# Head 0's cumulated sums by a transfer, the sum in two parts, and dummy matmuls by a running count

## The chip, the cores and the metric

The kernel runs on one core of a Trainium2 chip. A core has TensorE (PE in the profile; its weight loads are PEld), VectorE (DVE), ScalarE (ACT), GpSimd (POOL) and SyncE (SP), which here issues all transfers (DMA) from one queue in order. Each engine works through its own instructions in program order and waits on semaphores for the others. The metric is the device time of one execution in microseconds (us). [...]

## What is computed

Attention for 4 batches of 8 heads (576 positions, 64 wide) with a bias from cumulated sums, and then a mixture of four experts on the 2304 tokens:

```python
scores = scale * np.matmul(q, k.transpose(0, 1, 3, 2))
cum = np.cumsum(np.maximum(s, 0.0), axis=-1)
bias = -(cum[:, :, :, None] - cum[:, :, None, :])
scores = np.where(causal, -1000000000.0, scores + np.minimum(bias, 0.0))
attn = softmax(scores)
x = np.matmul(attn, v)             # then (B * S, H * D)
p = domain_probs / (domain_probs.sum(-1, keepdims=True) + 1e-09)
for e in range(E):
    h = np.maximum(x @ w1[e], 0.0)
    out += p[:, e:e + 1] * (h @ w2[e])
```

## The kernel before

**Order by a planner.** The program is straight-line code. Its first part (to about 320 us) is not written in the order in which it runs: `Sched.add` collects tasks with an estimated cost for each engine that could do them, dependences, a priority and buffers to take and give back, and `Sched.run` plays them through a model of the five engines (a clock `now` in ns, engines free from `T_START` on). Whichever task is free with the lowest priority number is emitted at that moment. So the order of instructions on each engine follows from planned times, and on the chip each engine keeps to that order.

**Attention.** `VISITS` lists 40 visits. Visits 0 to 7 take row blocks 0 to 2 (320 positions) of the first eight heads, visits 8 to 15 the remaining row blocks 3 and 4 of the same heads, visits 16 to 39 whole heads. Each visit loads q and k (L473, L480) into one of four buffers AB and v; each row block is a product S (L545), a minimum over it on VectorE (L562), an exponential on ScalarE (L570), the reciprocal of the sum (L576, L578), a normalisation, mostly on GpSimd (L375), transposes on TensorE (tile T, L599), copies out of PSUM (L380, L384), and a product with v (tile pv, L658). In visits 0 to 15 (`pq`) the product is one fp32 matmul over 66 rows: 64 of q and k, and two rows with the cumulated sums and constants, which a transfer (`ldc`, L490) brings from the tile `cx`. Its four rows hold ones, the sums (`cum`), the sums again (a ScalarE copy, L428), and -1. Visit 0 alone has no such transfer (`NDX = 1`): it multiplies 64 rows and adds the sums by two more matmuls per block, from `cum` and the identity (L547) and from `cum` and its negative, `nid` (L548).

The sums come from a scan on VectorE in two pieces, positions 0 to 319 and 320 to 575 (L426, L427), both ahead of every planned task. Two planned tasks (`t_chi` on ScalarE, `t_clo` on VectorE, priority `T_CE`) split the sums into a high and a low part, which `emit_ced` (L434) writes to memory for the visits from 16 on.

**Experts as filler.** Tasks of priority 1e6 and more are the matmuls of expert 0 (L746, L759, tile mo). TensorE takes them whenever no attention task is ready. They need the weights: eight blocks of 512 KB (L715) pass through two buffers `stage`, a copy on GpSimd or ScalarE (w1h, w2h) and a subtraction (w1l, w2l, L367). The remaining three experts follow after the attention phase in an order written out by hand.

**Dummies.** After 7 matmuls of ones in the start (`NWARM`, L404), `keep_warm` (L400) can place one dummy matmul of 192 columns into a free PSUM bank. The planner does so ahead of each attention task on TensorE, as long as fewer than `WCOLS` = 8 were placed in the last 3400 ns of planned time, and when TensorE has nothing to do after 3500. With the first expert matmul it ends for good:

```python
if e == "PE" and t.prio >= 1e6:
    self.warm = None
```

Of the kernel before, what the change touches and what calls it, by code (L numbers as in the profile page):

```python
# [11 lines left out]
F32 = mybir.dt.float32  # L12
# [81 lines left out]
DWQ = 0  # L94
DWL = 0
DWP = 1000
NDX = 1
NT_PR = 6000
T_CUM = 3800
T_CE = 6000  # L100
WMAX = 1
WCOLS = 8
T_START = (1500, 4200, 2000, 1700, 1100)
D1 = 700
LEND = {}
LAHEAD = 300
# [27 lines left out]
class Task:  # L134
    def __init__(self, engs, fn, deps, prio, take, give, xfer):
        self.engs = {e: c if isinstance(c, tuple) else (c, 0) for e, c in engs.items()}
        self.fn, self.prio, self.take, self.give, self.xfer = fn, prio, take, give, xfer
        self.wait = 0
        self.ready = 0.0
        self.next = []  # L140
        self.after = []
        self.done = None
        self.eng = None


class Sched:
# [38 lines left out]
    def run(self, until):  # L185
# [7 lines left out]
                for e in t.engs:  # L193
                    cand[e].append(t)
        now = 0.0
        recent = []
        while left:
            moved = False
            lend = not any(t.prio >= 1e6 and t.ready <= now + LAHEAD for t in cand["PE"])
            nxt = []  # L200
            for e in names:
                if free[e] > now:
                    nxt.append(free[e])
                    continue
                best = None
                for t in cand[e]:
                    if best is not None and t.key > best.key:
                        continue
                    if t.ready + t.engs[e][1] > now:
                        nxt.append(t.ready + t.engs[e][1])  # L210
                        continue
                    ok = True
                    for p, k in t.take:
                        f = min((b[0] for x in self.sources(t, p, lend) for b in self.pools[x]), default=1e18)
                        if f > now:
                            ok = False
                            if f < 1e17:
                                nxt.append(f)
                            break
                    if ok:  # L220
                        best = t
                if best is None:
                    if e == "PE" and self.warm and now > 3500:
                        x = self.warm(now)
                        if x:
                            recent.append(now)
                            free[e] = now + x
                            nxt.append(free[e])
                            moved = True
                    continue  # L230
                t = best
                extra = 0
                if e == "PE" and self.warm and t.prio < 1e6:
                    recent = [x for x in recent if x > now - 3400]
                    for _ in range(min(WMAX, WCOLS - len(recent))):
                        x = self.warm(now)
                        if x:
                            recent.append(now)
                            extra += x
                if e == "PE" and t.prio >= 1e6:  # L240
                    self.warm = None
                moved = True
                for x in t.engs:
                    cand[x].remove(t)
                for p, k in t.take:
                    x, b = min(((x, b) for x in self.sources(t, p, lend) for b in self.pools[x]), key=lambda y: y[1][0])
                    self.pools[x] = [y for y in self.pools[x] if y is not b]
                    self.tok[p, k] = b[1]
                    self.home[p, k] = x
                t.fn(e)  # L250
                end = now + extra + t.engs[e][0]
                free[e] = end
                if t.xfer is not None:
                    self.dma_free = max(self.dma_free, end + 700) + t.xfer / 330.0
                    end = self.dma_free + 900
                t.done, t.eng = end, e
                left.discard(id(t))
                for p, k in t.give:
                    self.pools[self.home.pop((p, k))].append([end + 150, self.tok.pop((p, k))])
                for n in t.after:  # L260
                    n.wait -= 1
                    if n.wait == 0:
                        for x in n.engs:
# [12 lines left out]


def body(ctx, tc, qk, vp, s, dp, w1, w1s, w2, w2s, out):
# [107 lines left out]

    s_sb = sch.pools["xr"][0][1][0:BH]
    cx = apool.tile([BH, 4, S], F32, name="cx")
    ones, cum = cx[:, 0], cx[:, 1]
    nid = const.tile([BH, BH], F32, name="nid")  # L390
    zero = const.tile([P, 1], F32, name="zero")
    warm = const.tile([P, 1], F32, name="warm")
    nc.sync.dma_start(out=s_sb, in_=s)
# [2 lines left out]
    def keep_warm(now):  # L396
        b = min((b for p in ("mo", "S", "T") for b in sch.pools[p]), key=lambda b: b[0], default=[1e18])
        if b[0] > now:
            return 0
        nc.tensor.matmul(b[1][:, 0:192], ones_bf[:, 0:128], ones_bf[:, 0:192], start=True, stop=True)  # L400
        return 83

    for _ in range(NWARM):
        nc.tensor.matmul(mo[1], ones_bf[:, 0:128], ones_bf, start=True, stop=True)  # L404
    nc.vector.memset(warm, 0.0)
    nc.gpsimd.memset(ones, 1.0)
    nc.gpsimd.memset(cx[:, 3], -1.0)
    nc.vector.memset(zero, 0.0)
    nc.scalar.activation(warm, warm, AF.Exp)
    make_identity(nc, idn)  # L410
    nc.gpsimd.tensor_scalar(nid, idn[0:BH, 0:BH], -1.0, 1.0, op0=ALU.mult, op1=ALU.mult)
# [10 lines left out]
    for _, t in sch.pools["osb"]:  # L422
        nc.vector.memset(t[:, 64:P], 0.0)
    s0 = rows(VA - 1)[1]
    for u, w in ((0, s0), (s0, S)):
        nc.vector.tensor_scalar(s_sb[:, u:w], s_sb[:, u:w], 0.0, 8.0, op0=ALU.max, op1=ALU.mult)  # L426
        nc.vector.tensor_tensor_scan(out=cum[:, u:w], data0=ones[:, u:w], data1=s_sb[:, u:w], initial=cum[:, u - 1:u] if u else 0.0, op0=ALU.mult, op1=ALU.add)  # L427
    nc.scalar.activation(cx[:, 2], cum, AF.Copy)  # L428

    c_hi, c_lo = aTh[0:BH, 0:S], aTl[0:BH, 0:S]  # L430

    def emit_ced(e):
        for r, t in ((0, ones), (1, ones), (2, c_hi.bitcast(F32)), (3, c_lo.bitcast(F32)), (4, cx[:, 3]), (5, cx[:, 3])):
            nc.sync.dma_start(out=ced[:, r], in_=t)  # L434

    t_chi = sch.add({"ACT": t_act(S, False)}, lambda e: hi(e, c_hi, cum), prio=T_CE)
    t_chi.ready = T_CUM
# [23 lines left out]
    for j, (h, ms) in enumerate(VISITS):  # L461
# [24 lines left out]
            ldv = sch.add({"SP": 500}, lambda e, j=j, h=h, nb=nb: nc.sync.dma_start(out=tok["vraw", j][:, 0:nb], in_=vp[h][:, 0:nb]),  # L486
                          [firstq.get(j - LV)], prio=base - 1300, take=[("vraw", j)], seq="vraw", xfer=nb * 128 * 64 * 4)
        ldc = None
        if pq and j >= NDX:
            ldc = sch.add({"SP": 500}, lambda e, j=j, h=h, ext=ext: nc.sync.dma_start(  # L490
                out=AB(j, F32)[64:66, :, 0:ext], in_=cx[h:h + 1, :, 0:ext].rearrange("p (r c) n -> p r c n", r=2)),
                prio=base - 1490, xfer=10000, follow=ld)
            ldc.ready = T_CUM + 600

        if first:
            qk_ready = [ld, ldc]
# [32 lines left out]
        for m in ms:  # L529
# [7 lines left out]
            for pi, (j0, j1) in enumerate(pieces):  # L537
                lastp = pi == len(pieces) - 1

                def f(e, j=j, a=a, j0=j0, j1=j1, c=c, pi=pi, ext=ext, pq=pq, h=h):  # L540
                    t = tok["S", (c, pi)]
                    if pq:
                        r = AB(j, F32)
                        k, w = 66 if j >= NDX else 64, min(P, ext - a)
                        nc.tensor.matmul(t[0:w, 0:j1 - j0], r[0:k, 0, a:a + w], r[0:k, 1, j0:j1], start=True, stop=k == 66)  # L545
                        if k == 64:
                            nc.tensor.matmul(t[0:w, 0:j1 - j0], idn[0:BH, h:h + 1].to_broadcast([BH, w]), cum[:, j0:j1], start=False, stop=False)  # L547
                            nc.tensor.matmul(t[0:w, 0:j1 - j0], cum[:, a:a + w], nid[:, h:h + 1].to_broadcast([BH, j1 - j0]), start=False, stop=True)  # L548
                    else:
                        for x, k in ((0, P), (1, 68)):  # L550
                            nc.tensor.matmul(t[:, 0:j1 - j0], AB(j)[0:k, x, a:a + P], tok["KK", j][0:k, x, j0:j1], start=(x == 0), stop=(x == 1))  # L551
                qt = sch.add({"PE": (t_pe4(j1 - j0) * (3 if j < NDX else 1) if pq else 2 * t_pe(j1 - j0))}, f, qk_ready + [last_q], prio=pr + pi, take=[("S", (c, pi))],
                             give=([("AB", j)] if pq else [("AB", j), ("KK", j)]) if lastp and m == ms[-1] else [])
                last_q = qt
                if j < NDX:
                    qt.ready = T_CUM - 150
                firstq.setdefault(j, qt)

                def f(e, m=m, n=n, a=a, j0=j0, j1=j1, c=c, pi=pi):
# [685 lines left out]
```

## Time and profile before

| | |
|---|---|
| median of three runs | 969.35 us (965.13 to 971.43) |
| the profiled execution, own time | 966.64 us |
| its span, first to last instruction | 964.9 us |
| mean granted clock of TensorE | 0.989 |
| busy: PE, DVE, ACT, POOL | 944.0, 734.5, 446.7, 450.0 us |

The profile is one execution. The span lies 1.7 us below the execution's own time, which includes what lies around it. A busy time of TensorE counts a slow matmul with its whole length, so the granted clock is to be read beside it.

### The profile page before, as it was taken

The numbers are of one execution on the slowest core, as the hardware profiler recorded it, in microseconds if no ns is written. First come the engines' busy times: TensorE is split into PE (matmuls) and PEld (weight loads), VectorE is DVE, ScalarE is ACT, GpSimd is POOL, SyncE is SP. The second block draws the span as 40 slices with busy tenths as digits, with TensorE's granted clock in tenths as the row PEclk, the third lists the DMA queues.
The fourth block names the chain that finished last, engine by engine and source line by source line (L and its number), as shares of the span: only waits on it lengthen the run. The fifth ranks groups of instructions, "written<-read, shape, count | busy, mean of one in ns | idle before, by whom it ended". The sixth has DMA issues, their size and how long they took to land.

```text
span 964.9 us, 18367 instructions
## 1 busy us (share of the span) xinstructions
PE 944.0 (98%) x6346; PEld 891.5 (92%) x6346; DVE 734.5 (76%) x1825; ACT 446.7 (46%) x1144; POOL 450.0 (47%) x505
## 2 busy tenths in 40 slices
PE   9989999999999999999999999999999999999998
PEld 6668889898898999999999999999999999999998
DVE  5879889889886222257688967997797979688976
ACT  4658787777775211244343344423343425343341
POOL 4456555655541389522381265317343624481222
PEclk7989999999999999999999999999999999999999
DMA  5857766757642596759645666555865468644613
GB/s 144 223 148 195 207 187 194 212 168 211 172 138 92 190 336 242 267 170 373 218 147 200 219 229 221 190 179 187 273 231 168 156 221 273 224 146 152 217 34 115
DMA packets 125975, 189.75 MB, mean 197 GB/s; under 512 B 10478, under 2 KB 102154, under 8 KB 125882
## 3 DMA queue, kind: packets, MB, share of 16 engines
q1 hardware_dynamic: 125882, 188.57, 61.0%
q8 instruction: 51, 0.84, 0.3%
q14 instruction: 42, 0.34, 0.1%
HBM read 144.73 MB, written 29.54 MB: 181 GB/s over the span
## 4 chain that ended last, share of the span: by engine, by line
PE 80%; DVE 11%; ACT 2%; DMA 2%; issue 2%; POOL 2%; DVEq 0%; SPq 0%; ACTq 0%; POOLq 0%
PE pb L1052 20%; PE pb L1044 19%; PE mo L1052 8%; PE mo L759 6%; PE mo L746 5%; PE T L599 5%; DVE w2l L367 4%; PE pv L658 4%; PE pb L746 4%; PE pb L759 3%; PE S L551 3%; PE S L545 2%; DMA x<-x_d 1%; DVE t L1086 1%; DVE a L562 1%
## 5 line engine op out<-in xcount | busy, mean ns | idle before, releaser
L1044 PE MATMUL pb<-x,w1h 128*128 128x384 f32 x1008 | 255.9, 334 | 0.5 <-ACT t L1082 0.5
L1044 PEld LDWEIGHTS pb<-x,w1h 128*128 128x128 f32 x1008 | 181.2, 188 | 0.9 <-ACT t L1082 0.8
L1044 PE MATMUL pb<-x,w1l 128*128 128x384 f32 x504 | 168.4, 334 | 0.0
L367 POOL TENSOR_TENSOR hT_r<-t,hT_r 128x768 fp32r<-128x768 f32 x18 | 33.9, 1885 | 273.8 <-ACT hT_r L380 177.4
L1082 ACT ACTIVATE t<-pb 128x384 f32<-128x384 f32 x144 | 67.0, 487 | 169.4 <-PE pb L1044 160.2
L1145 DVE SCALAR_TENSOR_TENSOR acc<-pb,prob,acc 128x256 f32<-128x256 f32 x288 | 126.2, 474 | 9.4 <-PE pb L1052 9.2
L375 POOL TENSOR_SCALAR a<-a,sm 64x64 f32<-64x64 f32 (+4 forms) x147 | 92.0, 630 | 67.2 <-DVE sm L578 39.6
L1052 PE MATMUL pb<-w2h,hT_r 128*128 128x256 f32 x720 | 115.7, 283 | 0.1
L570 ACT ACTIVATE a<-a,mx 64x64 f32<-64x64 f32 (+4 forms) x160 | 89.6, 562 | 26.9 <-DVE mx L562 16.5
L1052 PEld LDWEIGHTS pb<-w2h,hT_r 128*128 128x128 f32 x720 | 100.0, 191 | 0.5 <-DVE t L1086 0.3
L1059 ACT ACTIVATE hT_r<-t 128x768 fp32r<-128x768 f32 x54 | 45.7, 846 | 108.1 <-PE pb L1052 104.5
L1044 PEld LDWEIGHTS pb<-x,w1l 128*128 128x128 f32 x504 | 94.6, 188 | 0.0
L1086 DVE TENSOR_TENSOR t<-pb,t 128x384 f32<-128x384 f32 x108 | 56.2, 550 | 50.3 <-PE pb L1044 35.1
L1056 DVE SCALAR_TENSOR_TENSOR t<-t 128x768 f32<-128x768 f32 x72 | 88.0, 1223 | 2.2 <-ACT t L1082 2.1
L746 PE MATMUL mo<-xg,w1h 128*128 128x256 f32 (+1 forms) x344 | 80.5, 308 | 1.0 <-DVE xg L367 1.0
L599 PE MATMUL T<-idn,a 128*128 128x128 f32 x473 | 74.9, 281 | 6.7 <-POOL a L375 3.6
L380 ACT ACTIVATE aTh<-T 128x256 fp32r<-128x256 f32 (+2 forms) x278 | 65.6, 308 | 28.3 <-PE T L599 23.9
L1052 PE MATMUL pb<-w2l,hT_r 128*128 128x256 f32 x360 | 73.0, 284 | 5.1 <-DVE w2l L367 5.1
L635 DVE TENSOR_TENSOR aTl<-T,aTh 128x64 fp32r<-128x64 f32 (+3 forms) x247 | 72.6, 334 | 6.3 <-ACT aTh L380 5.2
L599 PEld LDWEIGHTS T<-idn,a 128*128 128x128 f32 x473 | 55.0, 143 | 21.1 <-issue 7.1
L562 DVE CUSTOM_DVE_ANT_0 a<-S,mask 128x192 f32<-128x192 f32 (+4 forms) x151 | 61.9, 419 | 3.9 <-PE S L545 1.9
L1145 DVE SCALAR_TENSOR_TENSOR acc<-mo,prob,acc 128x256 f32<-128x256 f32 x144 | 62.7, 474 | 1.6 <-PE mo L1052 1.6
(160 smaller groups left out, 2101.7 us busy)
## 6 DMA issues: line engine op xcount, KB each, us to landing
x<-xs_d SPq DMA_DIRECT2D x68, 768.0 KB
x<-x_d SPq DMA_DIRECT2D x55, 768.0 KB
xs_d<-x SPq DMA_DIRECT2D x12, 768.0 KB
raw<-in_qk_dram SPq DMA_DIRECT2D x24, 288.0 KB
KK<-AB_r SPq DMA_DIRECT2D x24, 288.0 KB
x_d<-xh SPq DMA_DIRECT2D x12, 576.0 KB
w1r<-in_w1s_dram SPq DMA_DIRECT2D x6, 1024.0 KB
w2r<-in_w2s_dram SPq DMA_DIRECT2D x6, 1024.0 KB
```

Source lines behind the costliest of these rows:

```text
L367: (nc.gpsimd if e == "POOL" else nc.vector).tensor_tensor(out=out, in0=in0, in1=in1, op=ALU.subtract)
L375: (nc.gpsimd if e == "POOL" else nc.vector).tensor_scalar(out, in_, scale, 1.0 if bias is None else bias, op0=ALU.mult, op1=ALU.mult if bi ...
L562: nc.vector.tensor_tensor_reduce(out=z[0:n, j0:j1], in0=tok["S", (c, pi)][0:n, 0:j1 - j0], in1=mask[0:n, 448 - a + j0:448 - a + j1], scale ...
L570: nc.scalar.activation(z[0:n, 0:bb], z[0:n, 0:bb], AF.Exp, bias=tok["mx", c][0:n, k:k + 1], scale=-1.0, accum_out=tok["sm", c][0:n])
L599: nc.tensor.transpose(t[:, 128 * k:128 * k + 128], z[:, 128 * x:128 * x + 128], idn)
L635: nc.vector.tensor_tensor(out=dst, in0=src, in1=h_.bitcast(F32), op=ALU.subtract)
L746: nc.tensor.matmul(t[:, 0:w], wl[q][:, dc, o:o + P], xgt[:, l, dc, 0:w], start=(u == 0), stop=(u == 3 * KD - 1))
L759: nc.tensor.matmul(t, ht[:, fc, 128 * ti:128 * ti + 128], wl[fc // 2][:, fc % 2, :], start=(u == 0), stop=(u == 3 * KF - 1))
L1044: nc.tensor.matmul(ts[u][:, 0:TG], wv[wl][:, k, 128 * u:128 * u + 128], x[:, xl_, k, :], start=start and k == 0 and n == 0, stop=k == 1 an ...
L1052: nc.tensor.matmul(ts[t][:, 0:256], h_part(o, hl_)[:, k, 128 * t:128 * t + 128], wv[wl][:, k, :], start=start and k == 0 and n == 0, stop= ...
L1056: (nc.gpsimd if e == "POOL" else nc.vector).scalar_tensor_tensor(out=out, in0=in0, scalar=0.0, in1=in1, op0=ALU.max, op1=op)
L1145: nc.vector.scalar_tensor_tensor(out=a_, in0=ts[t][:, 0:256], scalar=prob[:, tt, e:e + 1], in1=a_, op0=ALU.mult, op1=ALU.add)
```

## The change

Visit 0 gets its sums by the same transfer as the others, and `NDX`, `nid` and its two extra matmuls go. The scan's first piece (`cumulate(0, s0)`) and its copy stay ahead of the tasks; the second piece becomes planned tasks `t_cum2` (VectorE) and `t_cum3` (ScalarE) which are not planned before 12000 ns, and the transfers of visits 8 to 15 and `t_chi` depend on them. The dummy has 256 columns, and the planner places it by a running count: `active()` adds up TensorE's planned streaming over the last `HAM` ns, each task with a weight (0.9, products S of visits 0 to 15 with 0.5, dummies with 1.0). With nothing to do, TensorE gets a dummy while the count is under `FILL`; ahead of an attention task while it is under `KEEP`. This ends at `T_HAM` = 70000 ns of planned time. Engine start times and `T_CE`, `T_CUM` change too. The diff, its core:

```diff
-NDX = 1
-T_CUM = 3800
-T_CE = 6000
-WMAX = 1
-WCOLS = 8
-T_START = (1500, 4200, 2000, 1700, 1100)
+T_CUM = 4800
+T_CUM2 = 12000
+T_CE = 9000
+HAM = 3413
+KEEP = 0.45
+FILL = 0.6
+T_HAM = 70000
+T_START = (4000, 4300, 4700, 5200, 2600)
...
+        acts = [(800.0, T_START[0], 1.0)]
+
+        def active():
+            while acts and acts[0][1] <= now - HAM:
+                acts.pop(0)
+            return sum((min(y, now) - max(x, now - HAM)) * w for x, y, w in acts) / HAM
+
+        def dummy(at):
+            x = self.warm(at)
+            if x:
+                acts.append((at, at + x, 1.0))
+            return x
...
-                    if e == "PE" and self.warm and now > 3500:
-                        x = self.warm(now)
+                    if e == "PE" and self.warm and active() < FILL:
+                        x = dummy(now)
...
-                if e == "PE" and t.prio >= 1e6:
+                if e == "PE" and now > T_HAM:
                     self.warm = None
+                if e == "PE" and self.warm and t.prio < 1e6 and active() < KEEP:
+                    extra = dummy(now)
...
+                if e == "PE":
+                    acts.append((now + extra, end, t.act))
...
-        nc.tensor.matmul(b[1][:, 0:192], ones_bf[:, 0:128], ones_bf[:, 0:192], start=True, stop=True)
-        return 83
+        nc.tensor.matmul(b[1][:, 0:256], ones_bf[:, 0:128], ones_bf[:, 0:256], start=True, stop=True)
+        return 110
...
-    nc.scalar.activation(cx[:, 2], cum, AF.Copy)
+    def cum_again(u, w):
+        nc.scalar.activation(cx[:, 2, u:w], cum[:, u:w], AF.Copy)
+
+    cumulate(0, s0)
+    cum_again(0, s0)
+    t_cum2 = sch.add({"DVE": 1850}, lambda e: cumulate(s0, S), prio=T_CUM2 / 4)
+    t_cum2.ready = T_CUM2
+    t_cum3 = sch.add({"ACT": t_act(S - s0, False)}, lambda e: cum_again(s0, S), [t_cum2], prio=T_CUM2 / 4)
...
-        if pq and j >= NDX:
+        if pq:
...
+                          [None if first else t_cum3], prio=base - 1490, xfer=10000, follow=ld)
+            ldc.ready = T_CUM
...
-                            nc.tensor.matmul(t[0:w, 0:j1 - j0], idn[0:BH, h:h + 1].to_broadcast([BH, w]), cum[:, j0:j1], start=False, stop=False)
-                            nc.tensor.matmul(t[0:w, 0:j1 - j0], cum[:, a:a + w], nid[:, h:h + 1].to_broadcast([BH, j1 - j0]), start=False, stop=True)
...
+                qt.act = 0.5 if pq else 0.9
```

## Rows read from the trace of the kernel before

**Rows 1.** The page: chain that ended last by engine; granted clock in 40 slices.
```profile
PEclk7989999999999999999999999999999999999999
...
PE 80%; DVE 11%; ACT 2%; DMA 2%; issue 2%; POOL 2%; DVEq 0%; SPq 0%; ACTq 0%; POOLq 0%
```

**Rows 2.** Windows: stretch, length, busy PE, PEld, DVE, ACT, POOL (instructions), PEclk, DMA share, GB/s.
```profile
8.00:23.40 15.40, 15.40 (x59) 11.05 (x57) 7.37 (x50) 6.31 (x27) 5.47 (x10) 0.56 0.58 161
23.40:36.10 12.70, 12.55 (x90) 10.38 (x88) 12.15 (x53) 9.08 (x39) 5.08 (x6) 1.00 0.75 208
36.10:40.30 4.20, 2.84 (x20) 2.38 (x20) 2.43 (x9) 1.73 (x8) 3.04 (x3) 1.00 1.06 282
40.30:52.20 11.90, 10.90 (x56) 7.60 (x56) 8.99 (x33) 7.51 (x27) 6.54 (x9) 1.00 0.88 231
52.20:57.80 5.60, 2.35 (x15) 1.66 (x14) 5.00 (x12) 1.70 (x6) 3.93 (x5) 0.88 0.48 150
57.80:63.20 5.40, 5.37 (x22) 5.08 (x23) 3.02 (x13) 1.97 (x7) 2.20 (x3) 0.50 0.22 59
63.20:70.00 6.80, 6.60 (x40) 5.09 (x39) 5.93 (x21) 5.27 (x17) 2.69 (x7) 0.99 0.33 83
70.00:305.00 235.00, 230.95 (x1573) 206.90 (x1571) 208.47 (x819) 183.02 (x613) 128.60 (x278) 1.00 0.64 183
305.00:964.90 659.90, 649.74 (x4457) 637.28 (x4455) 476.01 (x801) 227.35 (x401) 288.10 (x167) 1.00 0.61 205
```

**Rows 3.** Chain that ended last at 70 us: start, length, engine, tile, line.
```profile
8.38 1.05 PE mo L547 x2
9.43 1.07 PE mo L548 x2
...
11.14 0.37 PE mo L545 x2
...
13.11 1.12 PE S L545 x2
...
38.05 0.20 PE S L545 x2
38.24 0.09 PE mo L400
38.33 0.37 PE S L545 x2
...
49.49 5.48 DMA stage<-in_w_dram
```

**Rows 4.** Waits, 0 to 70 us: in total, times, longest.
```profile
POOL w2h L382 <- DMA stage<-in_w_dram: 6.0, 4, 2.2
```

**Rows 5.** Timeline of the start: start, length, engine, line, operation [idle before <- releaser].
```profile
0.72 0.40 SPq L393 DMA_DIRECT2D xr<-in_s_dram  x1
...
1.18 0.75 SPq L473 DMA_DIRECT2D AB_f<-in_qk_dram  x1
...
2.60 0.69 DVE L426 TENSOR_SCALAR xr<-xr 32x320 f32<-32x320 f32 x1 [0.48 <-DMA xr<-in_s_dram]
...
3.41 0.81 DVE L427 TENSOR_TENSOR_SCAN cx<-cx,xr 32x320 f32<-32x320 f32 x1
...
4.15 1.07 DVE L426 TENSOR_SCALAR xr<-xr 32x256 f32<-32x256 f32 x1
...
4.63 0.50 PEld L545 LDWEIGHTS S<-AB_f 64*128 64x128 f32 x2 [0.30 <-DMA AB_f<-in_qk_dram]
...
5.25 0.74 DVE L427 TENSOR_TENSOR_SCAN cx<-cx,xr 32x256 f32<-32x256 f32 x1
...
6.03 0.68 ACT L428 ACTIVATE cx<-cx 32x576 f32<-32x576 f32 x1 [3.81 <-DVE cx L427]
...
7.32 0.74 DVE L367 TENSOR_TENSOR aTl<-cx,aTh 32x576 fp32r<-32x576 f32 x1 [1.32 <-ACT aTh L380]
```

**Rows 6.** The dummies' line L400: weight loads, min/median/max ns, first and last start.
```profile
L400 PEld LDWEIGHTS <-const-bfloat16-1.0 x51: 95/125/258, 3.3 to 38.4; 128*128 128x128 bf16 x51
```

More of the change, by code (lines that the diff above doesn't have):

```diff
@@ L143, in __init__ @@
         self.eng = None
+        self.act = 0.9
 class Sched:
@@ L195, in run @@
         now = 0.0
-        recent = []
+        acts = [(800.0, T_START[0], 1.0)]
[8 more added lines that the diff above has]
+            return x
         while left:
@@ L222, in run @@
                 if best is None:
-                    if e == "PE" and self.warm and now > 3500:
-                        x = self.warm(now)
+                    if e == "PE" and self.warm and active() < FILL:
+                        x = dummy(now)
                         if x:
-                            recent.append(now)
                             free[e] = now + x
@@ L229, in run @@
                             moved = True
+                    elif e == "PE" and self.warm:
+                        nxt.append(now + 100)
                     continue
@@ L232, in run @@
                 extra = 0
[L233 to L239, printed above, removed]
-                if e == "PE" and t.prio >= 1e6:
+                if e == "PE" and now > T_HAM:
                     self.warm = None
+                if e == "PE" and self.warm and t.prio < 1e6 and active() < KEEP:
+                    extra = dummy(now)
                 moved = True
@@ L388, in body @@
     cx = apool.tile([BH, 4, S], F32, name="cx")
-    ones, cum = cx[:, 0], cx[:, 1]
-    nid = const.tile([BH, BH], F32, name="nid")
+    ones, cum, minus = cx[:, 0], cx[:, 1], cx[:, 3]
     zero = const.tile([P, 1], F32, name="zero")
@@ L406, in body @@
     nc.gpsimd.memset(ones, 1.0)
-    nc.gpsimd.memset(cx[:, 3], -1.0)
+    nc.gpsimd.memset(minus, -1.0)
     nc.vector.memset(zero, 0.0)
@@ L410, in body @@
     make_identity(nc, idn)
-    nc.gpsimd.tensor_scalar(nid, idn[0:BH, 0:BH], -1.0, 1.0, op0=ALU.mult, op1=ALU.mult)
     nc.gpsimd.memset(mask, 0.0)
@@ L424, in body, with cumulate @@
     s0 = rows(VA - 1)[1]
-    for u, w in ((0, s0), (s0, S)):
+    def cumulate(u, w):
         nc.vector.tensor_scalar(s_sb[:, u:w], s_sb[:, u:w], 0.0, 8.0, op0=ALU.max, op1=ALU.mult)
         nc.vector.tensor_tensor_scan(out=cum[:, u:w], data0=ones[:, u:w], data1=s_sb[:, u:w], initial=cum[:, u - 1:u] if u else 0.0, op0=ALU.mult, op1=ALU.add)
-    nc.scalar.activation(cx[:, 2], cum, AF.Copy)
+    def cum_again(u, w):
[5 more added lines that the diff above has]
+    t_cum3 = sch.add({"ACT": t_act(S - s0, False)}, lambda e: cum_again(s0, S), [t_cum2], prio=T_CUM2 / 4)
     c_hi, c_lo = aTh[0:BH, 0:S], aTl[0:BH, 0:S]
     def emit_ced(e):
-        for r, t in ((0, ones), (1, ones), (2, c_hi.bitcast(F32)), (3, c_lo.bitcast(F32)), (4, cx[:, 3]), (5, cx[:, 3])):
+        for r, t in ((0, ones), (1, ones), (2, c_hi.bitcast(F32)), (3, c_lo.bitcast(F32)), (4, minus), (5, minus)):
             nc.sync.dma_start(out=ced[:, r], in_=t)
-    t_chi = sch.add({"ACT": t_act(S, False)}, lambda e: hi(e, c_hi, cum), prio=T_CE)
-    t_chi.ready = T_CUM
+    t_chi = sch.add({"ACT": t_act(S, False)}, lambda e: hi(e, c_hi, cum), [t_cum2], prio=T_CE)
     t_clo = sch.add({"DVE": t_dve(S), "POOL": (t_pool2(S), D3)}, lambda e: sub(e, c_lo, cum, c_hi.bitcast(F32)), [t_chi], prio=T_CE)
@@ L488, in body @@
         ldc = None
-        if pq and j >= NDX:
[L490 to L493, printed above, removed]
+        if pq:
+            ldc = sch.add({"SP": 500}, lambda e, j=j, h=h, ext=ext: nc.sync.dma_start(out=AB(j, F32)[64:66, :, 0:ext], in_=cx[h:h + 1, :, 0:ext].rearrange("p (r c) n -> p r c n", r=2)),
+                          [None if first else t_cum3], prio=base - 1490, xfer=10000, follow=ld)
+            ldc.ready = T_CUM
         if first:
@@ L543, in f @@
                         r = AB(j, F32)
-                        k, w = 66 if j >= NDX else 64, min(P, ext - a)
-                        nc.tensor.matmul(t[0:w, 0:j1 - j0], r[0:k, 0, a:a + w], r[0:k, 1, j0:j1], start=True, stop=k == 66)
-                        if k == 64:
-                            nc.tensor.matmul(t[0:w, 0:j1 - j0], idn[0:BH, h:h + 1].to_broadcast([BH, w]), cum[:, j0:j1], start=False, stop=False)
-                            nc.tensor.matmul(t[0:w, 0:j1 - j0], cum[:, a:a + w], nid[:, h:h + 1].to_broadcast([BH, j1 - j0]), start=False, stop=True)
+                        w = min(P, ext - a)
+                        nc.tensor.matmul(t[0:w, 0:j1 - j0], r[0:66, 0, a:a + w], r[0:66, 1, j0:j1], start=True, stop=True)
                     else:
@@ L551, in f @@
                             nc.tensor.matmul(t[:, 0:j1 - j0], AB(j)[0:k, x, a:a + P], tok["KK", j][0:k, x, j0:j1], start=(x == 0), stop=(x == 1))
-                qt = sch.add({"PE": (t_pe4(j1 - j0) * (3 if j < NDX else 1) if pq else 2 * t_pe(j1 - j0))}, f, qk_ready + [last_q], prio=pr + pi, take=[("S", (c, pi))],
+                qt = sch.add({"PE": (t_pe4(j1 - j0) if pq else 2 * t_pe(j1 - j0))}, f, qk_ready + [last_q], prio=pr + pi, take=[("S", (c, pi))],
                              give=([("AB", j)] if pq else [("AB", j), ("KK", j)]) if lastp and m == ms[-1] else [])
                 last_q = qt
-                if j < NDX:
-                    qt.ready = T_CUM - 150
+                qt.act = 0.5 if pq else 0.9
                 firstq.setdefault(j, qt)
```

## The prediction

> **What bounds the kernel now.** I read the page first. Its chain of work that ended last is 80% TensorE, and the clock row shows full speed everywhere but in the first and third slices of 24 us [rows 1]. [...]
>
> The windows by stage, second, say where it loses. From 70 us on TensorE is busy 230.95 of 235.00 and then 649.74 of 659.90 us at full clock [rows 2]; the change places nothing there. Since mixture-of-experts matmuls fill every TensorE gap of the attention phase, a shift of the pattern at 70 us should arrive at the end unchanged. That is an assumption; what it can cost is in the range.
>
> All that can be won lies before 70 us. The mean granted clock gives the time at the lower level: at a mean of 0.56 over 15.4 us it is (1 - 0.56) / 0.5 x 15.4 = 13.6 us, in one stretch; the second stretch is 0.88 over 5.6 us, 0.50 over 5.4 us and 0.99 over 6.8 us, so 1.3 + 5.4 + 0.1 = 6.9 us [rows 2]. In the first, TensorE is busy 15.40 of 15.40 us while VectorE is busy 7.37; in the next, VectorE is busy 12.15 of 12.70. Before the second, TensorE was busy only 2.35 of 5.60 us.
>
> The chain of waits, third, tells who sets the pace. Up to 23.4 us it is TensorE alone, and head 0 holds it for long: its third block ends with two cumulated-sum matmul pairs, 1.05 + 1.07 us, at 10.50 us; head 1 starts at 11.14 [rows 3]. Then VectorE paces to about 36 us. At 49.49 the chain waits 5.48 us for a transfer of expert weights [rows 3]; GpSimd waited four times for those, 6.0 us together [rows 4]. The transposes, and then TensorE, come behind that.
>
> **The change, part by part.**
>
> *Head 0 by a transfer.* Removed: the pairs of L547 and L548. Added: one small transfer of the sums' rows, after which head 0 is multiplied like the others. In the timeline of the start [rows 5] the first scan ends at 3.41 + 0.81 = 4.22. The copy on ScalarE now takes 320 columns instead of 576, 0.68 x 320/576 = 0.38 us, with a handover about 4.7. From issue to use the transfer of s took 2.60 - 0.72 = 1.88 us, that of head 0's q and k 4.63 - 1.18 = 3.45 us, so these sums land between 6.6 and 8.2; I take 7.0, since 5 KB are nearer to the small one. The two later transfers of the row wait in SP's queue behind it, and so do the loads of heads 2 and 3, which are not needed before 8 us. Head 0's three products at full clock are 0.20 and 0.37 us [rows 3], and half of the 1.12 us that 320 columns took at half clock: 1.13 us. They end at 8.1 to 8.2 where they ended at 10.50: 2.3 us earlier (1.1 to 2.7).
>
> *The sum in two parts.* The second half (1.07 + 0.74 = 1.81 us of VectorE, in the start at 4.15 and 5.25 [rows 5]) comes later, among the softmax work, and the 0.74 us subtraction of the split sums as well, which held VectorE at 7.32 after a wait for ScalarE. Behind the second half stand the row minima of heads 1 to 3. I count both against VectorE below. The result is first needed by the loads of visit 8, when the first heads are through; if it came later than that, every load behind that one in SP's queue would wait.
>
> *Dummies by a running count, in the first 36 us.* If the clock stays up, TensorE no longer paces: its work from 8.0 to 23.4 halves to about 8 us. VectorE does. Its work from 8.0 to 36.1 is 7.37 + 12.15 = 19.52 us [rows 2], and with 1.81 + 0.74 it is 22.07, starting at about 7.2. How densely it packs is not shown here: at best as in 23.4 to 36.1 (0.957), so 7.2 + 23.1 = 30.3 and 5.8 us are won; at worst TensorE still paces and only the start counts. I take the long attention row, 208.47 / 235.00 = 0.887 [rows 2]: 7.2 + 24.9 = 32.1, so 4.0 us are won at the 36.1 us mark (this contains the 2.3).
>
> *What is late next: the expert weights.* From 36.1 to 52.2 the DMA share is 1.06 and 0.88 [rows 2]; a stage that begins earlier does not get its 512 KB blocks earlier unless the queues had room. They had: 0.25 x 12.7 = 3.2 us in 23.4 to 36.1 and 0.12 x 11.9 = 1.4 us in 40.3 to 52.2. But two staging buffers chain each load to the split of the one before last. Of the 4.0 us between 0 and 4.0 pass; I take 3.0.
>
> *The second stretch at the lower clock.* Dummies now go on to 70 us of planned time instead of ending with the first expert matmul; the last of the 51 before started at 38.4 us [rows 6]. If they bridge 52 to 58 us, the 5.4 us in which TensorE was the bound at half clock (busy 5.37) shrink by half: 2.7 us. Bounds: 0, and 6.9 / 2 = 3.45.
>
> *What the dummies cost.* One of 192 columns took 0.09 us on the chain [rows 3]; one of 256 is then 0.12 us. Placed where the chip idles they cost nothing, and from 36.1 to 70 it idles 1.36 + 1.00 + 3.25 + 0.03 + 0.20 = 5.8 us, of which the rule fills 0.6, 3.5 us. They cost their full time where only the plan has a gap. I take 0.3 us, bounds 0 and 3.5. Each one also writes a bank and so waits for its last reader; in the row of the 51 I see nothing that waits for them. The cover is the plan's timing.
>
> *Sum.* 3.0 + 2.7 - 0.3 = 5.4 us. The profiled execution took 966.64 us (span 964.9), so 961.2 on its scale. It lies 2.7 us under the median of the three runs, 969.35 (965.13 to 971.43); the mean of all four is 968.1, and 968.1 - 5.4 = **962.7 us** is what I forecast.
>
> *A rule against it.* In 8.0 to 23.4 us TensorE was busy all of the time and yet had the lower clock [rows 2]: with products of 64 and 66 rows, transposes and a few dummies, busy time alone does not keep it up. The new count gives transposes the same 0.9 as full products. [...]
>
> **The rivals.**
>
> 1. *The count is wrong and the clock falls all the same.* For it: the full but slow stretch just told; the dummies are withheld at a count of 0.45 while products of 66 rows, counted at 0.5, run. Against: from 23.4 to 36.1 a mixture of the same products, transposes and dummies kept 1.00 [rows 2]. Only the earlier start is left, 2.3 us less 0.3: 966.1 us.
> 2. *The start's gain is lost at the expert weights.* For it: the DMA share of 1.06, four waits [rows 2, 4]. Against: the room before. Left are 2.7 - 0.3: 965.7 us.
> 3. *More is won.* VectorE packs at 0.957 (5.8 us), all 6.9 us go to full clock (3.45), and the TensorE gap of 52.2 to 57.8 closes (3.25 us): 12.5 us, 955.6. For it: the gap hangs on GpSimd's queue, where attention work stands behind a weight split that waits. Against: all three at once.
> 4. *Slower: dummies in front of real work.* The plan's gaps are not the chip's. Between 38.5 and 70 us the rule can place up to 0.6 x 31.5 = 18.9 us of dummies; on a TensorE that is really the bound (5.37 of 5.40 us) each costs 0.12 us. Above 5.7 us, some 47 of them, the kernel is slower than before; the full 18.9 give 968.1 - 5.7 + 18.9 = 981.3 us. For it: TensorE is in order and the expert matmuls need each slot. Against: the plan, too, has those matmuls as filler, so few gaps.
>
> **How the numbers follow.** The forecast has 0.40, rival 1 0.20, rival 2 0.15, rival 3 0.15, rival 4 0.10. The first three lie between 962.7 and 966.1; from run to run another 3 us come on top. Rival 4 (0.10), the far half of rival 3 and some spread are left out, under 0.2: range 955 to 970 us. One per cent of 969.35, 9.7 us, is about what a measurement can tell from no change. Below 959.7 lie most of rival 3 and a part of the forecast's high side: 0.20. Above 979.0 lies the bad half of rival 4, and some chance that a reshuffled plan loses elsewhere: 0.08. The rest, 0.72, is within 1%.
>
> **What would show it.** Head 0's first product at about 7.0 us and head 1's by 8.5; no L547 or L548. The granted clock at 1.00 in every window to 70 us; a window of 0.5 anywhere speaks for rival 1. VectorE's share from 8 to 32 us near 0.89. The waits for the weight transfers still there but ending some 3 us earlier (rival 2: at the same 55 us). Dummies after 38.5 us few, and in TensorE's idle time (rival 4: dozens, among expert matmuls). The windows from 70 us on should be the same work in the same length. I am wrong above all if TensorE's idle time between 70 and 305 us, now 4 us, changes by more than 2.

## The result, and the profile after

The changed kernel takes 953.13 us (median of five runs, 953.01 to 955.22) against 969.35 us before: a ratio of 0.9849 with a 95% interval of 0.9824 to 0.9874. It is 1.5% faster, three times the 5.4 us that were forecast, and lies under the range of 955 to 970 us. The profiled execution took 953.91 us, its span is 952.1 us; the span before was 964.9, so the two traces differ by 12.8 us.

The page of the changed kernel, its clock row and the chain by engine, answers [rows 1]:

```profile
PEclk9899999999999999999999999999999999999999
...
PE 75%; DVE 13%; ACT 3%; issue 3%; DMA 3%; POOL 2%; SPq 0%; DVEq 0%; ACTq 0%; POOLq 0%
```

The windows of the changed kernel, the same stretches and columns as [rows 2] (in the changed file L545 has become L562, L658 L671, L746 L759, L759 L772):

```profile
8.00:23.40 15.40, 13.60 (x79) 10.55 (x78) 13.19 (x64) 10.82 (x48) 9.90 (x15) 1.00 0.82 218
23.40:36.10 12.70, 11.15 (x48) 9.22 (x49) 10.26 (x52) 7.47 (x34) 6.30 (x8) 0.73 0.79 230
36.10:40.30 4.20, 4.20 (x24) 3.26 (x23) 2.66 (x12) 2.78 (x11) 2.22 (x4) 1.00 1.01 239
40.30:52.20 11.90, 9.69 (x62) 7.96 (x61) 10.30 (x31) 7.84 (x23) 6.38 (x10) 1.00 0.85 258
52.20:57.80 5.60, 5.60 (x42) 5.01 (x41) 4.92 (x15) 3.53 (x11) 2.38 (x5) 1.00 0.47 135
57.80:63.20 5.40, 5.40 (x38) 4.56 (x38) 5.29 (x20) 4.63 (x15) 3.70 (x6) 1.00 0.20 62
63.20:70.00 6.80, 5.39 (x35) 4.29 (x35) 6.34 (x20) 4.89 (x15) 3.88 (x8) 1.00 0.77 195
70.00:305.00 235.00, 231.50 (x1571) 207.44 (x1570) 203.23 (x806) 175.47 (x600) 129.15 (x271) 1.00 0.64 178
305.00:952.10 647.10, 637.45 (x4385) 626.78 (x4384) 471.37 (x787) 223.96 (x388) 288.17 (x167) 1.00 0.62 208
```

The clock column reads 1.00 in 8.00 to 23.40 here and 0.50 in 57.80 to 63.20 in [rows 2], and a mean between the two where it changes within a window; 0.50 is called the lower clock. Three things are to be seen. Both stretches at the lower clock are gone, and a shorter one has come: in 23.4 to 36.1 the mean is 0.73. From 70 us on nothing changed in kind: TensorE idles 3.50 us up to 305 where it idled 4.05. And TensorE's idle time as a whole is the same, 952.1 - 930.9 = 21.2 us against 964.9 - 944.0 = 20.9; it is its *busy* time that fell, by 13.1 us.

The dummies' line in the changed kernel (min/median/max ns, first and last start), beside [rows 6]:

```profile
L411 PEld LDWEIGHTS <-const-bfloat16-1.0 x16: 97/152/152, 3.3 to 14.9; 128*128 128x128 bf16 x16
L411 PE MATMUL mo<-const-bfloat16-1.0 x14: 272/420/421, 3.7 to 6.0; 128*128 128x256 bf16 x14
L411 PE MATMUL T<-const-bfloat16-1.0 x2: 273/273/273, 12.3 to 15.0; 128*128 128x256 bf16 x2
```

The running count placed 16 dummies where there had been 51: 14 in front of head 0's first product, two later, none after 15 us. The timeline of TensorE in the start:

```profile
3.70 2.58 PE L411 MATMUL mo<-const-bfloat16-1.0 128*128 128x256 bf16 x14
6.59 0.79 PE L562 MATMUL S<-AB_f 66*128 66x64 f32 x4 [0.31 <-DMA AB_f<-cx]
7.21 0.87 PE L562 MATMUL mo<-AB_f 66*128 66x320 f32 x4
7.92 1.08 PE L562 MATMUL S<-AB_f 66*128 66x192 f32 x4
9.11 0.79 PE L562 MATMUL mo<-AB_f 66*128 66x64 f32 x4
```

Head 0's first product waits for the transfer until 6.59 us. The row of 14 dummies that fills this wait, called the bridge below, ends 0.31 us earlier. By 9 us the products of two heads are through.

**An account of TensorE's time.** Since TensorE sets the end and its idle time did not change, I put its busy time together from its parts: time = work at full clock + half of the time at the lower clock + dummies + head 0's two extra products + idle time. The half is read from lengths on the chain of the kernel before: a dummy of 192 columns takes 0.16 us from 11.51 us, where the clock reads 0.50, and 0.08 us from 36.49, where it reads 1.00:

```profile
11.51 0.16 PE T L400
...
36.49 0.08 PE mo L400
```

The time at the lower clock is read from windows of 2 us, as 2 us x (1 - mean clock) / 0.5 each; a dummy of 192 columns counts as 0.08 us and one of 256 columns as 0.11 us (in the timeline of the changed kernel, one starts at 12.26 us and the next matmul at 12.37, where the clock reads 1.00). The extra products come from the chain of the kernel before; five pieces of it, the last four of them extra products beside the two in [rows 3]:

```profile
3.91 0.80 PE mo L400 x5
...
5.32 0.36 PE S L547 x2
5.68 0.22 PE S L548 x2
...
6.61 0.52 PE S L547 x2
7.13 0.33 PE S L548 x2
```

With 1.05 and 1.07 they are 3.55 us; the clock fell at about 8.67 (the window of 8.50 to 9.00 reads 0.66), so 1.83 us of them ran at half of it and count as 0.9: 2.6 us at full clock. One stretch at the lower clock stays out of the account. The windows read 1.00 from 0 us on, but the five dummies of 192 columns at 3.91 us take 0.16 us each, twice the 0.08, so the lower clock still held there; by 5.32 us the lengths are those of the full clock (0.36 us for the first pair of L547, 0.61 in e13 below). The changed kernel starts with such a stretch too (a dummy of its bridge takes 420 ns in the median, the two later ones 273); the others are taken to do so as well, and it is left in the last column. If the account is right, what is left, the work, must be the same in every variant. All profiles but that of e13, told below, in us:

| kernel | span | idle | at lower clock, half | dummies | extra products | left |
|---|---|---|---|---|---|---|
| before | 964.9 | 20.9 | 21.0, 10.5 | 51, 4.1 | 2.6 | 926.8 |
| changed | 952.1 | 21.2 | 8.0, 4.0 | 16, 1.8 | 0 | 925.1 |
| e1 | 969.6 | 27.5 | 22.8, 11.4 | 57, 4.6 | 0 | 926.1 |
| e2 | 958.3 | 20.6 | 14.5, 7.2 | 10, 1.1 | 2.6 | 926.8 |
| e3 | 957.6 | 24.7 | 14.6, 7.3 | 0 | 0 | 925.6 |
| e4 | 953.5 | 22.3 | 5.5, 2.8 | 27, 3.0 | 0 | 925.5 |
| e5 | 963.8 | 26.6 | 10.2, 5.1 | 45, 5.0 | 0 | 927.1 |
| e6 | 960.0 | 28.5 | 8.1, 4.0 | 16, 1.8 | 0 | 925.7 |
| e8 | 956.5 | 21.9 | 21.0, 10.5 | 0 | 0 | 924.1 |
| e9 | 961.1 | 22.2 | 21.7, 10.8 | 0 | 2.6 | 925.4 |
| e10 | 957.0 | 20.6 | 19.1, 9.6 | 15, 1.6 | 0 | 925.2 |
| e11 | 957.3 | 23.5 | 10.9, 5.5 | 15, 1.6 | 0 | 926.7 |
| e12 (before again) | 964.6 | 20.3 | 20.9, 10.4 | 51, 4.1 | 2.6 | 927.2 |

It closes to 924.1 to 927.2 in thirteen profiles. So the 12.8 us between the two traces are: lower clock 6.5, dummies 2.3, extra products 2.6, idle time -0.3, and 1.7 within the account's own spread. That spread is 3.1 us, so the account alone shows the clock's term; the terms of dummies and products are smaller than it, and for the dummies e8 and e9 below are the evidence.

### The profile page after: what moved, and what is told of

Read it like the earlier page. It is cut to its first block, busy times and chain, and to the rows that moved or that the text cites. A ratio compares the mean times of both kernels' runs of the same rounds, so it can differ in the third digit from the quotient of the medians.

```text
span 952.1 us, 18227 instructions
## 1 busy us (share of the span) xinstructions
PE 930.9 (98%) x6299; PEld 883.1 (93%) x6299; DVE 730.7 (77%) x1821; ACT 443.9 (47%) x1145; POOL 456.2 (48%) x508
## 4 chain that ended last, share of the span: by engine, by line
PE 75%; DVE 13%; ACT 3%; issue 3%; DMA 3%; POOL 2%; SPq 0%; DVEq 0%; ACTq 0%; POOLq 0%
PE pb L1065 20%; PE pb L1057 20%; PE mo L1065 8%; PE mo L759 5%; PE mo L772 4%; DVE w2l L379 4%; PE T L612 4%; PE pb L759 4%; PE pb L772 3%; PE pv L671 3%; PE S L565 2%; DMA x<-x_d 2%; DVE a L575 2%; DVE aTl L648 2%; DVE t L1099 1%
## 5 line engine op out<-in xcount | busy, mean ns | idle before, releaser
L387 POOL TENSOR_SCALAR a<-a,sm 128x576 f32<-128x576 f32 (+4 forms) x145 | 95.2, 661 | 65.4 <-DVE sm L591 50.9
L759 PE MATMUL mo<-xg,w1h 128*128 128x256 f32 (+1 forms) x344 | 79.9, 309 | 0.1
L392 ACT ACTIVATE aTh<-T 128x64 fp32r<-128x64 f32 (+2 forms) x278 | 66.6, 307 | 25.9 <-PE T L612 18.4
```

The lines of the kernel that those rows point to most:

```text
L387: (nc.gpsimd if e == "POOL" else nc.vector).tensor_scalar(out, in_, scale, 1.0 if bias is None else bias, op0=ALU.mult, op1=ALU.mult if bi ...
L759: nc.tensor.matmul(t[:, 0:w], wl[q][:, dc, o:o + P], xgt[:, l, dc, 0:w], start=(u == 0), stop=(u == 3 * KD - 1))
```

## The experiments

The ratios are to the kernel before in the same job on the same chip (its median there was 966.98 to 969.13 us), with 95% intervals; the changed kernel's is 0.9849 (0.9824 to 0.9874).

**e1: the new start with the old dummies.** Against the changed kernel (the core of the edit; the dummy has 192 columns again):

```diff
-                if e == "PE" and self.warm and t.prio < 1e6 and active() < KEEP:
-                    extra = dummy(now)
+                if e == "PE" and self.warm and t.prio < 1e6:
+                    recent = [x for x in recent if x > now - 3400]
+                    for _ in range(min(WMAX, WCOLS - len(recent))):
...
+                if e == "PE" and t.prio >= 1e6:
+                    self.warm = None
```

> The changed kernel, but with the dummies of the kernel before (192 columns, at most 8 in 3400 ns of planned time, over with the first expert matmul): the first head's transfer and the two-part sum alone. Theory 1, the running count keeps TensorE's clock up: without it the lower clock comes back between 9 and 22 us, about 13 us long, and the median is 960 to 966 us. Theory 2, the clock stays up because head 0's own sum products (rows of 32 and 64) are gone, and the count hardly matters: full clock to 22 us, and 953 us plus the time of 23 more dummies at 0.08 us, so 954 to 956.5 us.

Measured: 965.29 us (961.24 to 971.43), ratio 0.9977 (0.9957 to 0.9997). Neither theory. The clock did stay up to 34 us, as theory 2 had it, and the time is nevertheless in the band of theory 1. The plan placed 57 dummies, not the 39 I had counted on, 36 of them in front of head 0's first product, which begins at 7.26 us instead of 6.59. A stretch at the lower clock came later:

```profile
8.00:23.40 15.40, 14.43 (x99) 11.90 (x99) 12.82 (x67) 11.61 (x52) 9.61 (x15) 1.00 0.74 197
34.00:48.00 14.00, 12.95 (x40) 9.61 (x39) 6.76 (x24) 6.23 (x20) 8.33 (x13) 0.55 0.70 214
70.00:305.00 235.00, 226.69 (x1516) 201.56 (x1516) 202.65 (x798) 179.06 (x598) 127.26 (x273) 0.99 0.64 177
```

These are windows of e1. VectorE does 12.82 us of work in 8 to 23.4, nearly as in the changed kernel, so the attention phase did start early; the account shows where that went in the profiled execution: against the changed kernel 7.4 us more by the lower clock, 2.8 more of dummies, 6.3 more idle time. This is what overturned my theory that the first heads' pace sets the gain. The profiled execution is the longest of ten, with a mean clock of 0.988. The median is 6 us under it, and the shortest, 961.24 us, recorded 1.000; so much of this loss comes in some executions of the same program and not in others.

**e2: the new dummies with the old start.** The kernel before with `active()`, `KEEP`, `FILL`, `T_HAM` and the 256 columns; head 0 and the sum as before.

> The kernel before, with the running count for the dummies alone: head 0 keeps its two extra products per block, the sum is formed in one go. Theory 1: the first stretch at the lower clock (13.6 us) is gone or halved and the median is 955 to 961 us. Theory 2: the clock falls at about 9 us as before, and only the fewer dummies are won (51 of 0.08 to 0.16 us, about 4 us, against 33 of 0.11): 963 to 969 us.

Measured: 960.36 us, ratio 0.9932 (0.9911 to 0.9952). The clock falls at 8.5 us all the same (theory 2), but the time is that of theory 1. In the account: 3.0 us by dummies (10 instead of 51, and not the 33 I had stated) and 3.3 us because the stretch at 56 to 63 did not come, without a single dummy near it (the last is at 11.5 us).

**e3: no dummies at all.**

```diff
-    sch.warm = keep_warm
```

> The changed kernel without any dummy behind the seven of the start (the changed one has 16: 14 before head 0's first product, 2 after). Theory 1: TensorE idles from 4 to 6.6 us, the lower clock comes before 10 us and stays some 10 us; 957 us or more. Theory 2: head 0's first products start at the same 6.6 us, the clock stays up at least to 20 us, and the median is 952 to 955 us.

Measured: 959.70 us, ratio 0.9923 (0.9904 to 0.9941); theory 1's number, and its clock: 0.50 from 8 to 20 us, though head 0's first product begins at 6.58 us as in the changed kernel. But leaving the dummies out also changed the plan behind them, so the 6.6 us are not yet the dummies' alone. e8 settles that.

**e4: the sum in one go.**

```diff
-T_CUM = 4800
+T_CUM = 6700
...
     cumulate(0, s0)
-    cum_again(0, s0)
-    t_cum2 = sch.add({"DVE": 1850}, lambda e: cumulate(s0, S), prio=T_CUM2 / 4)
...
+    cumulate(s0, S)
+    cum_again(0, S)
+    t_cum2 = t_cum3 = None
```

> The changed kernel with the sum formed in one go ahead of the planned tasks (and the plan told of it: first transfer at 6700 instead of 4800 ns). Both theories: head 0's first product comes 1.8 to 2.0 us later (about 8.5 us). If the start's shift arrives at the end in full, 955 to 956 us; if the 1.81 us of VectorE that leave the softmax work make up for it, 953 us. Under theory 1 the longer bridge of dummies keeps the clock; under theory 2 it doesn't matter.

Measured: 958.20 us (955.72 to 958.77), ratio 0.9901 (0.9880 to 0.9921): 5 us more than the changed kernel, above both guesses. The first product is at 8.92 us, 2.33 later than 6.59; the bridge is then 9 dummies longer (23, and 4 come later). The profiled execution is the shortest of the four, so its row in the account does not hold the whole 5 us. How much of the 5 us is the later start and how much the other plan, no row splits.

**e8: the changed kernel's plan, its dummies not issued.** Each engine's order of everything else is the same.

```diff
-        nc.tensor.matmul(b[1][:, 0:256], ones_bf[:, 0:128], ones_bf[:, 0:256], start=True, stop=True)
         return 110
```

> The changed kernel's own plan, instruction for instruction, but none of its 16 dummies is issued (the plan still counts them). The run without dummies before this one had another plan as well and took 959.7 us, with the lower clock from 7 to 21 us. Theory A, TensorE's time at the lower clock is what costs: the clock falls at 7 us for some 13 us and the median is 958 to 961 us. Theory B, the order that the plan gave is what counts, and time at the lower clock only takes the place of idle time: the clock falls all the same, and the median is 952 to 955 us.

Measured: 958.19 us, ratio 0.9899 (0.9871 to 0.9928). Theory A. One window of e8, against that of the changed kernel above:

```profile
8.00:23.40 15.40, 14.87 (x48) 11.62 (x47) 7.89 (x52) 7.62 (x32) 4.76 (x11) 0.50 0.65 170
```

The clock is at half for the whole stretch, TensorE is full again (14.87 of 15.40) and VectorE's work falls from 13.19 to 7.89 us. In the account it loses 6.5 us by the clock and wins 1.8 by the dummies, 4.7 together; the medians, of two jobs, differ by 5.1. So in this plan 16 dummies, 14 of them where TensorE had nothing else to do, are worth 5 us.

**e9: the plan before, its 51 dummies not issued.** The same one-line edit in the kernel before.

> The kernel before with its own plan, but none of its 51 dummies is issued. Theory A: the 4.2 us of dummies are won and what more time at the lower clock costs is lost (it may now last from 8 to 25 us and come again up to 38 us): 964 to 972 us against 967. Theory B: the dummies stand in a stretch whose end is set by other things; 966 to 968 us whatever the clock does.

Measured: 962.86 us, ratio 0.9943 (0.9923 to 0.9962). Below both bands: leaving all dummies out made the *old* kernel 5.8 us faster than the 968.67 of that job. Part of that is the mixture of executions behind the 968.67 (told with e13 below): e9's profiled execution recorded a mean clock of 0.989, and against the three of that job with 0.986 to 0.989, 967.1 us in the mean, the gain is 4.2. Its windows of 8 to 23.4 and 36.1 to 52.2:

```profile
8.00:23.40 15.40, 15.31 (x54) 11.69 (x53) 8.77 (x54) 7.48 (x33) 5.50 (x10) 0.57 0.63 170
...
36.10:52.20 16.10, 12.63 (x66) 8.64 (x64) 12.30 (x39) 8.51 (x31) 9.12 (x11) 0.99 0.88 221
```

The mean clock in the first stretch is 0.57 without them and was 0.56 with them. The old dummies kept nothing up in the first stretch; they cost their 4.1 us, the part of them at half clock twice.

**e10, e11: how much is the plan's luck?** `T_CUM2` at 13000 and at 11000 instead of 12000.

```diff
-T_CUM2 = 12000
+T_CUM2 = 13000
```

> The changed kernel with the second half of the sum planned from 13000 instead of 12000 ns: the same work and nearly the same dummies, in a plan that differs from there on. Theory A: within 2 us of 953 unless a stretch at the lower clock comes or goes (half of its length each). Theory B: the plan's luck alone moves it, by 3 us or more, to 956 to 962 us, with the clock much as before.

> The same with 11000 ns. Theory A: within 2 us of 953 unless a stretch at the lower clock comes or goes. Theory B: 956 to 962 us with the clock much as before.

Measured: 955.41 us, 0.9864 (0.9829 to 0.9899), and 958.28 us, 0.9889 (0.9860 to 0.9918). The profiled executions have 19.1 and 10.9 us at the lower clock, at 22 to 27 and 32 to 47, and at 24 to 35 us. Both theories hold half: the differences are stretches at the lower clock (theory A), and they change with a constant that means nothing by itself (theory B). The plan alone does not fix them either: e10's profiled execution, with a mean clock of 0.990, is the longest of four, and the shortest recorded 0.997 and took 952.33 us, less than any execution of the changed kernel. The changed kernel has the best median of the three neighbours; 2 to 5 us of its gain may be of this kind, though the first interval overlaps its own.

**e5: more dummies.** Meant to beat the changed kernel by bridging 26 to 33 us.

```diff
-KEEP = 0.45
-FILL = 0.6
+KEEP = 0.6
+FILL = 0.8
```

> The changed kernel with the count's limits raised to KEEP 0.6 and FILL 0.8: more dummies, 45 instead of 16 (22 ahead of head 0's first product, most others between heads), in a plan that differs from there on. Account theory (time = 925 us of work at full clock + dummies + TensorE's idle time + half its time at the lower clock): if they bridge the stretch at 26 to 33 us, 3.4 us are won and 21 dummies of 0.11 us, 2.3 us, lost: 951 to 954 us, and the account closes to 924 to 927 us. If the higher count had to be better because the clock is, 950 us or less.

Measured: 964.04 us, ratio 0.9949 (0.9925 to 0.9973). A miss by 10 us, and the account closes (927.1): 45 dummies cost 5.0, stretches at 36 to 42 and 360 to 363 us came in place of that at 26 to 33, and TensorE idles 5.4 us more.

**e6: the weights' low parts on VectorE alone.**

```diff
-lo = sch.add({"DVE": (t_dve(n), DWL), "POOL": (t_pool2(n), DWP)}, lambda e, k=k, c0=c0, c1=c1: sub(
+lo = sch.add({"DVE": (t_dve(n), DWL)}, lambda e, k=k, c0=c0, c1=c1: sub(
```

(and the same for `t_clo`)

> The changed kernel with the low parts of expert 0's weights and of the sums computed by VectorE alone, never by GpSimd (in the changed kernel GpSimd runs one such subtraction of 1024 columns for 2.42 us at 19.9 and one of 576 for 2.37 us at 22.3, and VectorE's own at 20.1 takes 3.31 us instead of 1.22, after which TensorE idles half of 22 to 26 us and falls to the lower clock at 26). If the two engines are in each other's way there, VectorE's takes 1.22 us again, TensorE's gap and the stretch at 26 to 33 us go, and 3 to 5 us are won: 948 to 951 us. If the gap is a matter of the plan, it comes elsewhere: 953 to 958 us.

Measured: 958.84 us, ratio 0.9898 (0.9868 to 0.9928). Half a hit: the subtraction is quick again, and the stretch at 26 to 33 is gone, yet the kernel is slower. The gap came elsewhere: from 28 to 32 us TensorE is busy 0.69 of 4.00 us, and stretches at the lower clock follow at 34 to 37 and 82 to 85, 8.1 us in all as in the changed kernel (8.0). The low parts' line in e6 (min/median/max ns), and under it e6's long window:

```profile
L379 DVE TENSOR_TENSOR w1l<-stage,w1h x4: 1206/1217/1226, 20.1 to 35.9; 128x1024 fp32r<-128x1024 f32 x4
```

```profile
70.00:305.00 235.00, 225.32 (x1526) 203.24 (x1526) 203.20 (x795) 173.64 (x595) 123.90 (x273) 0.99 0.64 178
```

TensorE idles 9.7 us in 70 to 305 instead of 3.5, in another plan. So the slow subtraction was real, but what it costs the whole kernel is not shown: the plan changed with it.

**e12, e13: the kernel before, run twice more.**

> The kernel before, unchanged, to see a second execution's stretches. Executions with a mean clock of 0.996 took 968 to 971 us, those with 0.987 took 966 to 968. If time at the lower clock costs half of itself and nothing else differs, one with 0.996 should be 4 us shorter; so either TensorE idles some 6 us more in it, or the records of the clock miss a stretch (then products of 320 columns still take 1.1 us in it).

> The same once more: the stretch from 8 to 22 us at the lower clock again; the later one at 56 to 63 us may lie elsewhere or be missing. 966 to 971 us.

Measured: 966.41 us (mean clock 0.989) and 968.64 us (0.996). e12 repeats the first profile; e13 is the kind that is longer at a higher recorded clock. Such executions are common: of the 31 of the kernel before that ran beside the experiments, 17 recorded 0.985 to 0.989 and took 967.0 us in the mean, 14 recorded 0.994 to 0.998 and took 969.4. Windows of 2 us of e13, and under them pieces of its chain:

```profile
16.00:18.00 2.00, 2.00 (x8) 1.39 (x8) 0.79 (x5) 1.01 (x5) 0.74 (x2) 1.00 0.00 0
24.00:26.00 2.00, 2.00 (x10) 1.74 (x10) 0.00 (x0) 0.00 (x0) 1.05 (x1) 1.00 0.34 83
```

```profile
3.90 0.80 PE mo L400 x5
...
5.32 0.61 PE S L547 x2
...
15.84 1.12 PE S L545 x2
...
26.13 0.65 PE T L599 x3
```

The clock column says 1.00, but a product of 320 columns takes 1.12 us, its half-clock length [rows 3], and three transposes 0.65 us, where 0.33 is the full-clock length of three in the chain before. So the records miss the stretch: by the lengths the lower clock holds from the start to 26.8 us. The part from 5.3 on, 21.4 us, is what the first execution has not in its start, and with it the account gives 966.9 - 18.8 - (8.2 + 21.4) / 2 - 4.1 - 2.6 = 926.6, as in the others. It also says why this execution is longer than the first: there the clock rose by 5.32 us (L547 0.36 us), fell at 8.67 and rose again at 22.3; here it did not rise at 5.3 us (L547 0.61), and rose only at 26.8.

## Why the prediction was wrong

**What bounds the kernel**, TensorE, was right (80% of the chain before, 75% after), and so was the assumption that a gain before 70 us reaches the end: TensorE's idle time is 3.50 and 9.65 us in the two long stretches, 4.05 and 10.16 before.

**The step that failed** is the costing of the first stretch. I saw 13.6 us at the lower clock and then did not price it on TensorE: I let VectorE take over as the pace (4.0 us won at the 36.1 us mark) and the transfers of expert weights take a quarter of that away (3.0). But TensorE's freed time is not lost when VectorE paces attention, because expert matmuls fill it, and the plan can bring them forward. In the changed kernel they begin at 25.7 us instead of 38.5, and by 80 us 73 of them have started instead of 39. The larger part of both counts, before and after (min/median/max ns, first and last start):

```profile
L746 PE MATMUL mo<-xg,w1h x26: 278/364/499, 38.5 to 78.7; 128*128 128x256 f32 x26
L759 PE MATMUL mo<-xg,w1h x49: 278/283/562, 25.7 to 78.8; 128*128 128x256 f32 x49
```

VectorE's density was guessed well, 13.19 / 15.40 = 0.856 in 8 to 23.4 for 0.887, which shows that a right pace can stand in a wrong sum. Priced on TensorE, 6.5 us of the 12.8 are lower clock: 10.5 us before, 4.0 after. The first stretch's share is 3.4 (13.6 us at the lower clock have become 6.8, now at 26 to 33 us), and with the 2.6 us of extra products 6.0 stand where my sum had 3.0.

**The dummies had the wrong sign.** I charged 0.3 us for the new ones and credited nothing for the 51 old ones, although the sum said that TensorE was the bound there and I had their number and price side by side. They were worth 4.1 us; e9 measured 5.8 for leaving them out. The new ones take 1.8, almost all in time in which TensorE would idle. So the dummies gain 2.3 us where my sum let them lose 0.3.

**Head 0 by a transfer.** Right in time: the first product at 6.59 us (forecast 7.0, between 6.6 and 8.2), no L547 or L548. Its 2.3 us of earlier start were counted as part of the pace; the account has it as 2.6 us of removed products.

**The second stretch.** The 2.7 us were about right (3.4 by the account), but by luck, since the mechanism was not. I had dummies bridge 52 to 58 us; there are none after 15. The gap there is closed by expert matmuls, which the plan now has in it: TensorE is busy 5.60 of 5.60 us.

**The expert weights.** GpSimd still waited for them, 4.6 us instead of 7.3, and the loads started between 12.9 and 46.1 us instead of 15.0 and 49.5. The waits did not bind as I feared: expert 0's first layer needs only its first four blocks. Rival 2 did not happen.

**Rival 1**, "the clock falls all the same". It did once in the changed kernel, at 26 us, and read 0.52 in the 7 us behind. In the 4 us before it TensorE was busy only 2.07 of 4.00 us, which suggests the gap. But a gap alone does not settle it: from 48 to 52 us TensorE was busy even less, 1.79 of 4.00, and the clock stayed at 1.00 behind it. Nor is it shown whether transposes deserve the same 0.9 in the count as full products, since no run here separates them. It stays open.

```profile
22.00:26.00 4.00, 2.07 (x12) 1.43 (x11) 4.00 (x18) 1.36 (x7) 2.67 (x2) 0.99 0.74 192
26.00:33.00 7.00, 7.00 (x26) 6.09 (x26) 5.23 (x29) 3.68 (x17) 3.48 (x5) 0.52 0.81 244
...
48.00:52.00 4.00, 1.79 (x11) 1.16 (x9) 3.05 (x6) 2.08 (x6) 3.61 (x3) 1.00 0.61 187
```

These are windows of the changed kernel around that fall and at the other gap.

**Rival 3**, "more is won", came nearest (955.6 us), in part for other reasons than those listed. Of its three one holds, the second stretch at full clock. The gap at 52 to 58 us closed, but TensorE's idle time only moved (21.2 us in all for 20.9). VectorE did not pack at 0.957 (0.856). The dummies left out, 2.3 us, were not among them.

**What is settled and what is not.** Shown: the dummies of the changed kernel are worth 5 us (e8), those of the old one cost 4 to 6 (e9), and busy time is made of these parts to within 3 us (the account). In the profiled executions the clock of the start hangs on both edits. With the old start it falls at 7.6 to 8.7 us under either rule for the dummies and without any (before, e2, e9; in e13 it never rose before 26.8); with the new start and no dummies it falls at 7.1 to 7.8 (e3, e8); with the new start and dummies of either rule it stays up past 23 (changed, e1, e4, e5, e6, e10, e11). What in the old start lets it fall is not shown. Nor is it shown how much each *edit* brings to the time alone: the start alone gives 0.9977, the dummies alone 0.9932, both 0.9849, and every edit reshuffles the plan, which by e10 and e11 moves 2 to 5 us and by e6 and e5 more. The median's distance of 16.2 us is larger than that of the two traces because the profiled execution before was one of the shorter ones; e13 shows what a longer one has, a start that never left the lower clock until 26.8 us.

## What to carry to other kernels

Where one engine is never idle because filler waits for it, price a change on that engine alone: what it no longer streams, plus what its time at the lower clock costs (here half of it, at a reading of 0.50), plus its idle time, and check that the rest is the same before and after. Here dummy matmuls were worth their place where the engine would idle: 16, of which 14 stood in one gap before the first product, brought 5 us, while 51 in another start, most of them spread through the work, cost 4 to 6. In a kernel whose order comes from a planner, try neighbours of each constant, and several executions of each, before crediting a gain to an edit.

## What the runs showed of the hardware

- The granted clock in the profile of e13 misses a whole stretch: it reads 1.00 in the windows from 8 to 26 us while the products of 320 columns take 1.12 us, as in the kernel before at 0.50 [rows 3], and three transposes 0.65, where they take 0.33 in the kernel before at 1.00. The first profile of this kernel reads 1.00 from 0 to 5 us too, over dummies of 0.16 us. The length of a known matmul was the safer reading here.
- From 8 to 23.4 us TensorE was busy 15.31 to 15.40 of 15.40 us with a mean clock of 0.56 to 0.57, so 13.2 to 13.6 us of it at the lower clock (before, e2, e9). In the changed kernel, after 14 dummies in a row up to 6.3 us, products of 66 rows ran at 1.00 until 26 us.
- Beside a subtraction on GpSimd, one on VectorE took longer. In the timeline of the changed kernel GpSimd's runs from 19.91 to 22.33, VectorE's begins at 20.10 and takes 3.31 us where it takes 1.22 alone; in e6, with VectorE alone on such work, all four take 1.21 to 1.23.

```profile
19.91 2.42 POOL L379 TENSOR_TENSOR w1l<-stage,w1h 128x1024 fp32r<-128x1024 f32 x1
20.10 3.31 DVE L379 TENSOR_TENSOR w1l<-stage,w1h 128x1024 fp32r<-128x1024 f32 x1
...
22.29 2.37 POOL L379 TENSOR_TENSOR aTl<-cx,aTh 32x576 fp32r<-32x576 f32 x1
```
